# Seven quarter-block products for the second FFN product of the last five chunks, and token tiles that wait in DRAM

## The chip, the cores and the metric

One core of a Trainium2 chip runs the whole program in one launch. The metric is device time in microseconds (us), the median of the runs; lower is better. TensorE (PE) multiplies matrices into PSUM, VectorE (DVE) and ScalarE (ACT) read PSUM and SBUF, GpSimd (POOL) works on SBUF, and SyncE's queue (SP) issues all the DMAs of this kernel.

## What is computed

Attention with 32 pooled memories per head, then a Fourier mix over tokens and channels, then a normalised feed-forward network (FFN) with a residual:

```
a = softmax(phi over tokens);  k_m, v_m = a^T k, a^T v          # 32 memories per head
x = softmax(q k_m^T / 8) v_m                                    # (8, 576, 512)
u = x + real(fft(fft(x, tokens), channels))
un = (u - mean(u)) / sqrt(var(u) + 1e-6)
out = u + relu(un @ w_ch1) @ w_ch2                              # 512 -> 2048 -> 512
```

There are 8 batches of 576 tokens, so 4608 tokens, or 36 tiles of 128.

## The kernel before

**Two streams.** The FFN works on chunks of CH = 2 tiles (256 tokens): 18 chunks, 0 to 17, each in NW = 8 steps j of 256 hidden units. Beside it runs a generator, `background`, that makes the mixed token tiles `u` batch by batch: pooling, scores, spectrum `at`, values `vh`, and the products `pp` and `px` (`mix_m`, `mix_x`, `add_mix`). It yields 14 times per batch, and `advance` (L1134) runs it one part further per step of the FFN, as long as the ring of NU = 8 tiles (`uring`) has room; a tile is freed when its chunk is done.

**Numbers in halves.** From chunk 1 on every fp32 factor is split into an fp16 value and an fp16 rest, and a product is three matmuls: value by value, value by rest, rest by value.

**One step of the FFN.** `ffn1` (L846) makes 256 hidden units for 256 tokens: 24 matmuls of 128x256 into `ph` (they appear at L288, the line of the recording helper), then ACT writes relu as fp16 into `hring` (L864) and DVE the rest (L865). `ffn2` (L870, matmul at L874) multiplies them with `w2s`: 12 matmuls of 128x512 into two PSUM tiles `po`, one per token tile, each over all 512 output columns. ffn1 runs NHS = 7 steps ahead of ffn2. After step 7 `finish` (L882) adds `po` to `u` on DVE (L886) and sends the tile out (L887); `norm_chunk` (L792) normalises chunk c+2: ACT (L781, L782, L807), POOL (L787, and L808 for the fp16 rest `ud`), DVE (L783 to L788), and a DMA transpose into `unring`.

**Order.** A scheduler of the build sets the order of the instructions on each engine from the order of the program and its own estimate; on the chip each engine takes its queue strictly in that order and waits on semaphores. What two engines do at a time is not fixed otherwise.

```
for n in range(NW, n_steps):
    c, j = divmod(n, NW)
    ffn2(c, j, hs[c], po)
    run_ffn1(n + NHS)
    if j < NW - 1:
        advance(CH * c, steps=1)
    else:
        finish(c, po)
        if c + 2 < n_chunks:
            advance(CH * (c + 1), CH * (c + 3))
            unTs[c + 2] = norm_chunk(c + 2)
```

The functions that the diff touches, with the line numbers of the profile:

Of the kernel before, what the change touches and what calls it, by code (L numbers as in the profile page):

```python
# [10 lines left out]
F32 = mybir.dt.float32  # L11
F16 = mybir.dt.float16
# [3 lines left out]
AF = mybir.ActivationFunctionType  # L16
ALU = mybir.AluOpType
# [114 lines left out]
def kernel(  # L134
# [11 lines left out]

    const = ctx.enter_context(tc.tile_pool(name="const", bufs=1))
    psg = ctx.enter_context(tc.tile_pool(name="psg", bufs=4, space=PSUM))
    ps1 = ctx.enter_context(tc.tile_pool(name="ps1", bufs=2, space=PSUM))
    ps2 = ctx.enter_context(tc.tile_pool(name="ps2", bufs=2, space=PSUM))  # L150

# [91 lines left out]
    kept = []  # L243
# [582 lines left out]
    def h_slot(c, j):  # L826
        return hring[:, (4 + c * NW + j) % NW]
# [18 lines left out]
    def ffn1(c, unT, j, hs):  # L846

        ph = ps1.tile([P, UB, CH, P], F32, tag="h", name=f"ph_{c}_{j}")
        mm = groups()
        for f in range(UB):  # L850
            i = 0
            for k in range(NK):
                for lw, lu in ((0, 0), (0, 1), (1, 0)):
                    mm(
                        ph[:, f],
                        lhsT=w1t[:, j, lw, k, f * P : (f + 1) * P],
                        rhs=unT[:, lu, :, k],
                        start=(i == 0),
                        stop=(i == 3 * NK - 1),
                    )  # L860
                    i += 1
        h = h_slot(c, j)
        phv = ph.rearrange("p f t c -> p (f t) c")
        nc.scalar.activation(h[:, 0], phv, AF.Relu)  # L864
        nc.vector.scalar_tensor_tensor(  # L865
            out=h[:, 1], in0=phv, scalar=0.0, in1=h[:, 0], op0=ALU.max, op1=ALU.subtract
        )
        hs.append(h)

    def ffn2(c, j, hs, po):  # L870
        for f in range(UB):
            for t in range(CH):
                for i, (lh, lw) in enumerate(((0, 0), (0, 1), (1, 0))):
                    nc.tensor.matmul(  # L874
                        po[t],
                        lhsT=hs[j][:, lh, f * 2 + t],
                        rhs=w2s[:, j * UB + f, lw, :],
                        start=(j == 0 and f == 0 and i == 0),
                        stop=(j == NW - 1 and f == UB - 1 and i == 2),
                    )  # L880

    def finish(c, po):  # L882
        for t in range(CH):
            idx = CH * c + t
# [116 lines left out]
    n_chunks = n_tiles // CH  # L1001

    allocs = []

    def background():

        nt = 0
        u2, half_made = None, None
        for b in range(B):
            n = f"{b}"  # L1010
            ivs = tiny("ivs", NG)
            mem, ahl = {}, {}
            if b != 1:
                pooling_weights(b)
            yield (nt if half_made is None else half_made), 0
            if b == 0:

                for g in range(NG + 1):
                    if g < NG:
                        km = memory_f32(b, g, first[g], vmf, [0])  # L1020
                        mem[g] = first[g][:, KV:], None, km, 1.0 / 8.0
                    if g > 0:
                        ahl[g - 1] = pair_scores(b, g - 1, *mem.pop(g - 1), aeo)
                for g in range(NG):
# [17 lines left out]
            vbd = vbdt.rearrange("p (l g) f -> p l g f", l=2)  # L1042
            for g in sorted(ahl):
                pair_transpose(b, g, ahl.pop(g), attnT)
            full = slice(0, P)
            for t in (0, 1, 2) if b % 2 == 0 else (2, 0, 1):
                yield (nt if half_made is None else half_made), 2 if t < 2 else 1 - b % 2
                if t == 2:
                    if b % 2 == 0:
                        u2 = uring[:, len(allocs) % NU]  # L1050
                        us[nt] = u2
                        allocs.append(nt)
                        half_made = nt
                        nt += 1
                    rows = slice(64 * (b % 2), 64 * (b % 2) + 64)
                    tm = mix_m(b, "t2", slice(256, 320), rows, at, vh, isg, isq)
                    px = mix_x(b, "t2", 4 * P + 64, 64, rows, attnT, vbd)
                    add_mix(u2, rows, px, igx, tm, 0)
                    half_made = nt - 1 if b % 2 == 0 else None
                    continue  # L1060
                tm = mix_m(b, f"t{t}", slice(t * P, (t + 1) * P), full, at, vh, isg, isg)
                for sign in range(2):
                    c0 = (2 * t + sign) * P
                    px = mix_x(b, f"t{t}{sign}", c0, P, full, attnT, vbd)
                    u = uring[:, len(allocs) % NU]
                    allocs.append(nt)
                    add_mix(u, full, px, igx, tm, sign)
                    us[nt] = u
# [113 lines left out]
    unTs[2] = norm_chunk(2)  # L1182
    for n in range(NW, n_steps):
        c, j = divmod(n, NW)
        if j == 0:
            po = [ps2.tile([P, 512], F32, tag="o", name=f"po_{c}_{t}") for t in range(CH)]
        ffn2(c, j, hs[c], po)
        run_ffn1(n + NHS)
        if j < NW - 1:
            advance(CH * c, steps=1)  # L1190
        else:
            finish(c, po)
            if c + 2 < n_chunks:
# [66 lines left out]
```

## Time and profile before

| what | us |
|---|---|
| median of 3 runs (lowest to highest) | 943.62 (942.4 to 962.26) |
| the profiled execution's own time | 943.25 |
| its span, from the first to the last instruction | 941.4 |
| PE busy in the span | 931.6 |

A duration in the rows is that of one instruction on its engine, waiting on another engine's use of a shared resource included. Matmuls are pipelined: the duration of one is longer than the distance to the next, so rates are read from runs of many. "Idle before" is the time in which the engine stood still ahead of a group, with what ended it. POOL spans are rough.

### The profile page before, as it was taken

Reading aid. Unit: us, or ns where it says so; the run is one execution under the profiler, and the core shown is the slowest. Engines: PE = TensorE matmul, PEld = TensorE weight load, DVE = VectorE, ACT = ScalarE, POOL = GpSimd, SP = SyncE. Lnnn points to the kernel's source line nnn. Section 1 sums busy time; section 2 is a strip of 40 time slices with the busy share of each in tenths; the row PEclk is TensorE's granted clock in tenths of the full one; section 3 lists DMA queues with packets and bytes.
Section 4 is the critical chain, followed back from the end, with each engine's and each line's share of the span. In section 5 each row is a group of like instructions: output and inputs, shape, how many; then the busy total and the mean of one; then the engine's idle time right before and its main releaser. Section 6 shows DMA issues by size and latency. Waiting matters only on the chain.

```text
span 941.4 us, 18994 instructions
## 1 busy us (share of the span) xinstructions
PE 931.6 (99%) x7820; PEld 666.2 (71%) x7820; DVE 548.0 (58%) x1271; ACT 459.6 (49%) x920; POOL 217.5 (23%) x255
## 2 busy tenths in 40 slices
PE   9999899999999999999999999999999999999998
PEld 8977577676777777676767767777776767666664
DVE  5989957576656666667514766667656675221111
ACT  5668858655465536554514554656446444311110
POOL 1313424142212314223100331323122231200000
PEclk9999899999999999999999999999999999999999
DMA  9957521642235412553104531373124211110000
GB/s 328 383 217 245 184 85 24 124 123 68 53 75 123 105 42 46 141 111 93 24 23 86 115 103 42 59 162 98 26 68 85 72 25 47 23 46 23 1 24 22
DMA packets 115959, 88.09 MB, mean 94 GB/s; under 512 B 100384, under 2 KB 100384, under 8 KB 113824
## 3 DMA queue, kind: packets, MB, share of 16 engines
q1 hardware_dynamic: 115872, 86.87, 34.7%
q8 instruction: 61, 1.00, 0.4%
q14 instruction: 26, 0.21, 0.1%
HBM read 58.15 MB, written 9.44 MB: 72 GB/s over the span
## 4 chain that ended last, share of the span: by engine, by line
PE 88%; DVE 3%; ACT 1%; issue 1%; POOL 0%; DVEq 0%; ACTq 0%
PE ph L288 38%; PE po L874 37%; PE pm L288 2%; PE pp_t L288 2%; PE px_t L288 2%; PE psc L288 1%; PE po L838 1%; PE pa L684 1%; DVE w2s L930 1%; PE ph L821 1%; PE pv L657 1%; PE pp_t L727 1%; PE pf L362 1%; DVE w1t L930 0%; ACT elt L941 0%
## 5 line engine op out<-in xcount | busy, mean ns | idle before, releaser
L288 PE MATMUL ph<-unring,w1t 128*128 128x256 f16 x3264 | 388.9, 273 | 0.0
L874 PE MATMUL po<-w2s,hring 128*128 128x512 f16 x1632 | 378.8, 379 | 0.0
L288 PEld LDWEIGHTS <-w1t 128*128 128x128 f16 x3264 | 315.0, 98 | 64.4 <-issue 3.3
L874 PEld LDWEIGHTS <-hring 128*128 128x128 f16 x1632 | 156.8, 98 | 158.0 <-issue 0.4
L865 DVE SCALAR_TENSOR_TENSOR hring<-ph,hring 128x512 f16<-128x512 f32 x136 | 93.1, 685 | 155.4 <-ACT hring L864 154.8
L864 ACT ACTIVATE hring<-ph 128x512 f16<-128x512 f32 x136 | 80.3, 591 | 161.3 <-PE ph L288 160.9
L592 POOL TENSOR_TENSOR aring<-aring,scratch 128x384 f32<-128x384 f32 x28 | 23.3, 833 | 212.2 <-DVE scratch L590 208.6
L787 POOL TENSOR_TENSOR scratch<-scratch,small 128x1 f32<-128x1 f32 x36 | 21.7, 608 | 168.2 <-DVE scratch L786 135.1
L288 PEld LDWEIGHTS <-stg 128*128 128x128 f16 x1152 | 44.8, 98 | 8.4
L586 ACT ACTIVATE aring<-aring,scratch 128x384 f32<-128x384 f32 x24 | 14.7, 612 | 71.0 <-DVE aring L585 71.0
L808 POOL TENSOR_TENSOR ud<-un,ud 128x1024 f16<-128x1024 f32 x17 | 36.2, 2129 | 29.6 <-ACT ud L807 27.7
L509 POOL TENSOR_TENSOR stg<-rawt,stg 128x640 f16<-128x640 f32 x12 | 17.7, 1475 | 90.2 <-ACT rawt L508 90.2
L838 PE MATMUL po<-w2s,hring 128*128 128x512 f32 x64 | 32.8, 637 | 4.3 <-ACT hring L824 4.2
L611 ACT CAST aeo<-eo 128x384 f16<-128x384 f32 x30 | 15.3, 511 | 41.4 <-DVE eo L608 41.4
L886 DVE SCALAR_TENSOR_TENSOR uring<-po,small,uring 128x512 f32<-128x512 f32 x34 | 24.0, 742 | 17.6 <-PE po L874 17.6
L576 DVE TENSOR_REDUCE scratch<-psc 128x12 f32<-128x384 f32 x32 | 17.6, 549 | 28.5 <-PE pm L288 16.1
L763 DVE SCALAR_TENSOR_TENSOR uring<-px_t,scratch,share 128x256 f32<-128x256 f32 (+1 forms) x80 | 33.9, 475 | 0.2 <-PE px_t L288 0.2
L602 POOL TENSOR_TENSOR aring<-aring 128x128 f32<-128x128 f32 x56 | 32.8, 605 | 2.1
L604 DVE TENSOR_TENSOR eo<-aring 128x128 f32<-128x128 f32 x29 | 29.5, 1018 | 5.9 <-POOL aring L602 5.9
L288 PE MATMUL pm<-et,stg 128*128 128x64 f16 (+1 forms) x740 | 32.0, 195 | 0.0
L821 PE MATMUL ph<-unring,w1t 128*128 128x256 f32 x128 | 32.0, 395 | 0.0
L749 DVE SCALAR_TENSOR_TENSOR share<-pp_t,scratch,small 128x257 f32<-128x257 f32 (+1 forms) x48 | 21.0, 480 | 18.1 <-ACT small L746 18.0
(263 smaller groups left out, 1212.3 us busy)
## 6 DMA issues: line engine op xcount, KB each, us to landing
out<-uring SPq DMA_DIRECT2D x36, 256.0 KB, 2.1
rawt<-in_raw SPq DMA_DIRECT2D x13, 640.0 KB, 4.9
stg<-in_raw SPq DMA_DIRECT2D x13, 640.0 KB, 4.8
stg<-in_w SPq DMA_DIRECT2D x7, 1024.0 KB, 6.0
rawt<-in_raw SPq DMA_DIRECT2D x15, 384.0 KB, 3.3
stg<-in_raw SPq DMA_DIRECT2D x15, 384.0 KB, 3.1
phs<-in_raw SPq DMA_DIRECT2D x28, 160.0 KB, 3.8
w2s<-in_w SPq DMA_DIRECT2D x4, 1024.0 KB, 10.8
```

Source lines behind the costliest of these rows:

```text
L288: m = nc.tensor.matmul(out, lhsT=lhsT, rhs=rhs, start=start, stop=stop)
L592: eng.tensor_tensor(out=a, in0=a, in1=sm.unsqueeze(2).to_broadcast([P, 12, M]), op=ALU.mult)
L602: eng.tensor_tensor(out=a2[:, i : i + 4], in0=a[:, 0:4], in1=a[:, 4:8], op=op)
L604: nc.vector.tensor_tensor(out=eo[:, 1:3, 0], in0=ap[:, 1:3, 0], in1=ap[:, 1:3, 1], op=ALU.add)
L763: nc.vector.scalar_tensor_tensor(out=u[rows, hs], in0=px[rows, hs], scalar=igx[rows], in1=tm[rows, w * NJ + half : w * NJ + half + 256], o ...
L808: marks[f"ul{c}"] = nc.gpsimd.tensor_tensor(out=ud[:, 1], in0=un, in1=ud[:, 0], op=ALU.subtract)
L821: nc.tensor.matmul(ph, lhsT=w[:, k, f * P : (f + 1) * P], rhs=unTs[0][:, k], start=(k == 0), stop=(k == NK - 1))
L838: nc.tensor.matmul(po[t], lhsT=h[:, f, t], rhs=w[:, f], start=(j == 0 and f == 0), stop=(j == NW - 1 and f == UB - 1),)
L864: nc.scalar.activation(h[:, 0], phv, AF.Relu)
L865: nc.vector.scalar_tensor_tensor(out=h[:, 1], in0=phv, scalar=0.0, in1=h[:, 0], op0=ALU.max, op1=ALU.subtract)
L874: nc.tensor.matmul(po[t], lhsT=hs[j][:, lh, f * 2 + t], rhs=w2s[:, j * UB + f, lw, :], start=(j == 0 and f == 0 and i == 0), stop=(j == NW ...
L886: nc.vector.scalar_tensor_tensor(out=u, in0=po[t], scalar=cout if c else 0.5, in1=u, op0=ALU.mult, op1=ALU.add)
```

## The change

Three things are done together.

1. **Seven products.** For chunks 13 to 17 (from C0 on) the second product is written with 2 x 2 blocks: the two token tiles by the two 128-unit halves of a step, against the two halves by two blocks of 256 output columns. Instead of eight block products there are seven, of sums and differences of blocks (the scheme of Strassen in Winograd's form). A step then has 21 matmuls of 128x256 (L960) in place of 12 of 128x512. The factors have to be made: four sums of blocks of `w2s` for each j, once (`prepare_sums` on POOL, L910 to L915; `split_sums`, a copy on ACT, L920, and a subtraction on DVE, L921), and four sums of blocks of relu(ph) for each step (`ffn1_sums`: relu on ACT, L927, four 128x128 operations on DVE, L929, a 128x896 copy on ACT, L930, and a 128x896 subtraction on DVE, L931). `finish_sums` puts the seven products together (L977, L979, L983 to L987). In chunk 17 the products p2, p4 and p3 of steps 4 to 7 come last.
2. **Tiles in DRAM.** Mixed tiles from number 10 on are written to one of two slots of `uring`, sent to `kept_u` in DRAM (`keep`, L1129), and fetched for their chunk (`fetch`, L1135), so that the ring no longer stops the mixing. `due` gives it one part per step, eight per chunk instead of seven, and it must be through at the end of chunk 11.
3. **Places.** The operands of 1 lie in buffers of the mixing: the fp16 weight sums `t_slots` in `stg` and `rawt`, the sums of activations `s_slots` in `phs`, `et`, `aeo`, `attnT` and `hring`, two fp32 buffers `sums` in `aring` and `vh`, and two fp32 buffers `t_sums` for the weight sums in `at` and `uring[:, 2:4]`. ffn1 runs NS - 1 = 6 steps ahead from chunk 13 on.

```
+    t_sums = [flat(at, "a c").bitcast(F32)[:, : 2 * DM].rearrange("p (f c) -> p f c", f=UB), uring[:, 2:4]]
...
+        if c >= C0:
+            hs.append(ffn1_sums(c, j, ph))
+            return
...
+    def prepare_sums(j):
+        w, t, N = w2s[:, j * UB : (j + 1) * UB], t_sums[j % 2], DM // 2
+        nc.gpsimd.tensor_tensor(out=t, in0=w[:, :, 0], in1=w[:, :, 1], op=ALU.add)
+        b11, b12, b21, b22 = (t[:, f, n * N : (n + 1) * N] for f in range(2) for n in range(2))
+        nc.gpsimd.tensor_tensor(out=b11, in0=b12, in1=b11, op=ALU.subtract)
+        nc.gpsimd.tensor_tensor(out=b12, in0=b22, in1=b12, op=ALU.subtract)
+        nc.gpsimd.tensor_tensor(out=b22, in0=b22, in1=b11, op=ALU.subtract)
+        nc.gpsimd.tensor_tensor(out=b21, in0=b21, in1=b22, op=ALU.subtract)
+    def split_sums(j):
...
+        nc.scalar.copy(out=hi, in_=tf)
+        nc.vector.tensor_tensor(out=lo, in0=tf, in1=hi, op=ALU.subtract)
+    def ffn1_sums(c, j, ph):
+        m = (c - C0) * NW + j
+        a, h = sums[m % 2], s_slots[m % NS]
+        nc.scalar.activation(a[:, 0:4], ph.rearrange("p f t c -> p (f t) c"), AF.Relu)
+        for o, x, y, op in ((6, 1, 0, ALU.subtract), (4, 0, 2, ALU.add), (5, 2, 6, ALU.subtract), (7, 3, 5, ALU.subtract)):
+            nc.vector.tensor_tensor(out=a[:, o], in0=a[:, x], in1=a[:, y], op=op)
+        nc.scalar.copy(out=h[:, 0], in_=a[:, 1:8])
+        nc.vector.tensor_tensor(out=h[:, 1], in0=a[:, 1:8], in1=h[:, 0], op=ALU.subtract)
...
+        factors = {
+            "p1": (0, plain(0, 0)),
+            "p6": (4, summed(3)),
...
+        for n in names:
+            a, b = factors[n]
+            for i, (la, lb) in enumerate(((0, 0), (0, 1), (1, 0))):
+                    m = nc.tensor.matmul(po[n], lhsT=h[:, la, a], rhs=b[lb],
...
+    def keep(nt, u, rows):
+        if nt >= KEPT:
+            nc.sync.dma_start(out=kept_u[nt, rows], in_=u[rows])
...
+            ffn2_sums(j, hs[c][j], po, FIRST if late else FIRST + SECOND)
...
+        if 0 < n - (C0 - 1) * NW <= NW:
+            split_sums(n - (C0 - 1) * NW - 1)
+        if c == C0 - 1:
+            prepare_sums(j)
+        run_ffn1(n + (NHS if n + NHS <= C0 * NW else NS - 1))
+        if made < n_tiles:
+            due += PACE
```

On POOL the last rows of the mixing, of which the kernel before has these ahead of its last tiles' normalisation (aring and aeo hold the scores, L787 and L808 belong to the normalisation):

```order
L592 TENSOR_TENSOR aring<-aring,scratch 128x384
L602 TENSOR_TENSOR aring<-aring 128x128 x2
L600 TENSOR_TENSOR ahring<-aring,ahring 128x5x64
L612 TENSOR_TENSOR aeo<-eo,aeo 128x8x32
L787 TENSOR_TENSOR scratch<-scratch,small 128x1
L808 TENSOR_TENSOR ud<-un,ud 128x1024
```

are followed in the changed kernel by the weight sums of j = 0 alone (in `at`) and then of two j at a time (in `uring` and `at`):

```order
L634 TENSOR_TENSOR aeo<-eo,aeo 128x8x32
L910 TENSOR_TENSOR at<-w2s 128x1024
L912 TENSOR_TENSOR at<-at 128x256
L913 TENSOR_TENSOR at<-at 128x256
L914 TENSOR_TENSOR at<-at 128x256
L915 TENSOR_TENSOR at<-at 128x256
L910 TENSOR_TENSOR uring<-w2s 128x1024
L912 TENSOR_TENSOR uring<-uring 128x256
L910 TENSOR_TENSOR at<-w2s 128x1024
L913 TENSOR_TENSOR uring<-uring 128x256
```

So 40 new POOL instructions stand in one row at the seam of chunks 12 and 13, and the normalisation of chunk 14 (two L809, one L830) stands among them.

On DVE the end of a chunk late in the kernel before reads as follows: one row per step for the rest of the activations (L865) and two rows that finish the chunk (L886).

```order
L865 SCALAR_TENSOR_TENSOR hring<-ph_3_9654,hring 128x512
L865 SCALAR_TENSOR_TENSOR hring<-ph_4_9693,hring 128x512
L886 SCALAR_TENSOR_TENSOR uring<-po_0_9369,small,uring 128x512
L886 SCALAR_TENSOR_TENSOR uring<-po_1_9370,small,uring 128x512
L865 SCALAR_TENSOR_TENSOR hring<-ph_5_9732,hring 128x512
```

At the seam of chunks 12 and 13 the changed kernel has these (et, aeo and attnT hold the activations of chunk 13, steps 1 to 3; stg takes the weight sums of j = 0 to 2; po_0 and po_1 are those of chunk 12):

```order
L929 TENSOR_TENSOR vh<-vh 128x128 x4
L931 TENSOR_TENSOR et<-vh,et 128x896
L921 TENSOR_TENSOR stg<-at,stg 128x1024
L929 TENSOR_TENSOR aring<-aring 128x128 x4
L931 TENSOR_TENSOR aeo<-aring,aeo 128x896
L929 TENSOR_TENSOR vh<-vh 128x128 x4
L998 SCALAR_TENSOR_TENSOR uring<-po_0_8825,small,uring 128x512
L921 TENSOR_TENSOR stg<-uring,stg 128x1024
L998 SCALAR_TENSOR_TENSOR uring<-po_1_8826,small,uring 128x512
L931 TENSOR_TENSOR attnT<-vh,attnT 128x896
L921 TENSOR_TENSOR stg<-at,stg 128x1024
```

One DVE row per step has become five, and at this seam six; the finish of chunk 12 (L998) and the weight rests (L921) share the queue with them.

## Rows read from the trace of the kernel before

**Rows 1.** The page: the span, and each engine's busy time, its share of the span and its instructions.

```profile
span 941.4 us, 18994 instructions
PE 931.6 (99%) x7820; PEld 666.2 (71%) x7820; DVE 548.0 (58%) x1271; ACT 459.6 (49%) x920; POOL 217.5 (23%) x255
```

**Rows 2.** Busy time of each engine in stretches of the span: the stretch, its length, then busy us (and instructions) of PE, PE's weight loads, DVE, ACT and POOL, then PE's granted clock, the DMA share and GB/s.

```profile
250.00:340.00 90.00, 90.00 (x826) 63.60 (x824) 56.56 (x133) 48.73 (x99) 25.83 (x29) 1.00 0.39 88
680.00:770.00 90.00, 90.00 (x823) 63.32 (x821) 55.94 (x132) 46.43 (x95) 23.35 (x25) 1.00 0.28 64
815.00:920.00 105.00, 105.00 (x730) 71.27 (x729) 18.75 (x27) 12.54 (x21) 0.00 (x0) 1.00 0.07 21
```

**Rows 3.** The chain of work that ended last, in order of time (start, us, what), at the end of the mixing, in a late chunk, and at the end of the span.

```profile
796.11 0.89 PE px_t L288 x16
797.00 6.69 PE po L874 x31
803.69 5.24 PE ph L288 x48
...
838.68 2.59 PE po L874 x12
841.27 2.62 PE ph L288 x24
...
922.04 14.91 PE po L874 x69
936.95 0.03 issue
936.97 0.75 DVE uring L886
```

**Rows 4.** Groups of instructions on PE: line, engine, operation, out<-in, shapes, count, then busy us and mean ns of one, then idle time before them.

```profile
L288 PE MATMUL ph<-unring,w1t 128*128 128x256 f16 x3264 | 388.9, 273 | 0.0
L874 PE MATMUL po<-w2s,hring 128*128 128x512 f16 x1632 | 378.8, 379 | 0.0
L288 PEld LDWEIGHTS <-w1t 128*128 128x128 f16 x3264 | 315.0, 98 | 64.4 <-issue 3.3
```

**Rows 5.** Instructions by line on POOL, ACT and DVE: count, then the shortest, middle and longest duration in ns, first and last start, and shapes.

```profile
L602 POOL TENSOR_TENSOR aring<-aring x56: 449/457/1053, 86.8 to 773.5; 128x128 f32<-128x128 f32 x56
L592 POOL TENSOR_TENSOR aring<-aring,scratch x28: 831/832/835, 85.9 to 772.2; 128x384 f32<-128x384 f32 x28
L808 POOL TENSOR_TENSOR ud<-un,ud x17: 2123/2130/2140, 72.7 to 810.7; 128x1024 f16<-128x1024 f32 x17
L787 POOL TENSOR_TENSOR scratch<-scratch,small x36: 549/551/1068, 50.5 to 808.0; 128x1 f32<-128x1 f32 x36
L807 ACT CAST ud<-un x17: 1028/1045/1055, 71.6 to 809.5; 128x1024 f16<-128x1024 f32 x17
L604 DVE TENSOR_TENSOR eo<-aring x29: 273/866/1473, 26.3 to 774.0; 128x128 f32<-128x128 f32 x29
L562 DVE SCALAR_TENSOR_TENSOR stg<-rawt,scratch,stg x12: 1005/1018/1470, 173.1 to 741.8; 128x768 f16<-128x768 f32 x12
L993 DVE SCALAR_TENSOR_TENSOR w2s<-w2s,small x5: 1273/1276/1817, 141.1 to 169.8; 128x1024 f16<-128x1024 f32 x5
L865 DVE SCALAR_TENSOR_TENSOR hring<-ph,hring x136: 626/690/693, 133.5 to 922.7; 128x512 f16<-128x512 f32 x136
L763 DVE SCALAR_TENSOR_TENSOR uring<-px_t,scratch,share x80: 441/474/501, 47.2 to 798.7; 128x256 f32<-128x256 f32 x64, 64x256 f32<-64x256 f32 x16
```

**Rows 6.** DVE and POOL in order of time around 190 us: start, us, engine, line, operation, out<-in, shapes, count, and in brackets the idle time before it.

```profile
188.47 0.83 POOL L592 TENSOR_TENSOR aring<-aring,scratch 128x384 f32<-128x384 f32 x1 [13.12 <-DVE scratch L590]
188.84 1.27 DVE L562 SCALAR_TENSOR_TENSOR stg<-stg,scratch 128x768 f16<-128x768 f32 x1 [0.52 <-ACT stg L561]
189.38 1.46 POOL L602 TENSOR_TENSOR aring<-aring 128x128 f32<-128x128 f32 x2
...
190.80 1.39 POOL L509 TENSOR_TENSOR stg<-stg 128x640 f16<-128x640 f32 x1
190.87 1.47 DVE L604 TENSOR_TENSOR eo<-aring 128x128 f32<-128x128 f32 x1 [0.36 <-POOL aring L602]
```

**Rows 7.** PE around the one long wait of the span: in order of time, and then its busy time and granted clock (the third number) in stretches.

```profile
109.83 3.78 PE L838 MATMUL po<-w2s,hring 128*128 128x512 f32 x4 [3.69 <-ACT hring L824]
...
110.00:113.00 3.00, 3.00 (x4) 0.50 0.00 0
113.00:116.00 3.00, 3.00 (x8) 0.51 0.28 55
116.00:119.00 3.00, 3.00 (x19) 1.00 0.40 117
```

**Rows 8.** DMA issues: out<-in, queue, kind, count, KB each, median us from issue to landing.

```profile
out<-uring SPq DMA_DIRECT2D x36, 256.0 KB, 2.1
```

More of the change, by code (lines that the diff above doesn't have):

```diff
@@ L51 @@
 NW = NF // UB
+C0 = 13
+NS = 7
+PACE = 1.0
+KEPT = 10
 UW = UB * DM
@@ L58 @@
 W2_STAGE = ["b10", "b14", "s2", "b10", "b14", "x", "s2", "s1"]
+FIRST, SECOND = ["p1", "p6", "p7", "p5"], ["p2", "p4", "p3"]
 HEADS = [0, 1, 2, 3, 7, 6, 5, 4]
@@ L148 @@
     psg = ctx.enter_context(tc.tile_pool(name="psg", bufs=4, space=PSUM))
+    kept_u = ctx.enter_context(tc.tile_pool(name="kept", bufs=1, space=bass.MemoryType.DRAM)).tile(
+        [B * S // P, P, DM], F32, name="kept_u"
+    )
     ps1 = ctx.enter_context(tc.tile_pool(name="ps1", bufs=2, space=PSUM))
@@ L219, with flat @@
     share = const.tile([P, 2 * NJ], F32, name="share")
+    def flat(t, names):
+        return t.rearrange(f"p {names} -> p ({names})")
+    t_slots = [stg[:, i, k * 2048 : (k + 1) * 2048] for i in (0, 2) for k in range(2)]
+    t_slots += [rawt.bitcast(F16)[:, k * 2048 : (k + 1) * 2048] for k in range(2)]
+    t_slots += [stg[:, 1, k * 2048 : (k + 1) * 2048] for k in range(2)]
+    t_slots = [t.rearrange("p (l b c) -> p l b c", l=2, b=4) for t in t_slots]
+    s_slots = [flat(phs, "t g c").bitcast(F16), flat(et, "g l t c"), flat(aeo, "l t e h c"), flat(attnT, "g t c")]
+    s_slots += [flat(hring[:, i : i + 2], "a l f c") for i in (4, 6, 0)]
+    s_slots = [t[:, : 14 * P].rearrange("p (l b c) -> p l b c", l=2, b=7) for t in s_slots]
+    sums = [flat(aring, "a t m")[:, : 8 * P], flat(vh, "l k c").bitcast(F32)]
+    sums = [t.rearrange("p (b c) -> p b c", b=8) for t in sums]
+    t_sums = [flat(at, "a c").bitcast(F32)[:, : 2 * DM].rearrange("p (f c) -> p f c", f=UB), uring[:, 2:4]]
     rings, taken = {}, [0]
@@ new lines, in split_sums @@
+    def split_sums(j):
+        hi, lo = (t_slots[j][:, l].rearrange("p b c -> p (b c)") for l in range(2))
+        tf = t_sums[j % 2].rearrange("p f c -> p (f c)")
+        nc.scalar.copy(out=hi, in_=tf)
[8 more added lines that the diff above has]
+        nc.vector.tensor_tensor(out=h[:, 1], in0=a[:, 1:8], in1=h[:, 0], op=ALU.subtract)
+        return h
@@ new lines, in sums_banks, with ffn2_sums, plain, summed @@
+    def sums_banks(c):
+        banks = [ps2.tile([P, 512], F32, tag="o", name=f"po_{c}_{i}") for i in range(2)]
+        banks += [psg.tile([P, 512], F32, tag="g", name=f"po_{c}_{2 + i}") for i in range(2)]
+        names = ("p1", "p2"), ("p6", "p7"), ("p5", "p3"), ("p4",)
+        return {n: banks[i][:, k * 256 : (k + 1) * 256] for i, p in enumerate(names) for k, n in enumerate(p)}
+    def ffn2_sums(j, h, po, names):
+        def plain(f, n):
+            return [w2s[:, j * UB + f, l, n * 256 : (n + 1) * 256] for l in range(2)]
+        def summed(b):
+            return [t_slots[j][:, l, b] for l in range(2)]
+        factors = {
+            "p1": (0, plain(0, 0)),
+            "p6": (4, summed(3)),
+            "p7": (5, summed(1)),
+            "p5": (3, summed(0)),
+            "p2": (2, plain(1, 0)),
+            "p4": (1, summed(2)),
+            "p3": (6, plain(1, 1)),
+        }
+        for n in names:
+            a, b = factors[n]
+            for i, (la, lb) in enumerate(((0, 0), (0, 1), (1, 0))):
+                with tc.issue_after(marks["ps"].ins) if i == 0 and "ps" in marks else nullcontext():
+                    m = nc.tensor.matmul(
+                        po[n],
+                        lhsT=h[:, la, a],
+                        rhs=b[lb],
+                        start=(j == 0 and i == 0 and n in ("p1", "p6", "p5", "p4")),
+                        stop=(j == NW - 1 and i == 2),
+                        skip_group_check=True,
+                    )
+            marks["ps"] = m
@@ new lines, in finish_sums, with add @@
+    def finish_sums(c, po):
+        u2, u1 = us.pop(CH * c), us.pop(CH * c + 1)
+        lo, hi = slice(0, 256), slice(256, 512)
+        c1, x1 = share[:, 0:256], share[:, 256:512]
+        x2, x3 = (elt.rearrange("p l c -> p (l c)").bitcast(F32)[:, i * 256 : (i + 1) * 256] for i in range(2))
+        def add(o, p, x):
+            nc.vector.scalar_tensor_tensor(out=o, in0=po[p], scalar=cout, in1=x, op0=ALU.mult, op1=ALU.add)
+        nc.scalar.activation(c1, po["p1"], AF.Copy, scale=cout)
+        add(x1, "p6", c1)
+        add(x2, "p7", x1)
+        add(x3, "p5", x1)
+        nc.gpsimd.tensor_tensor(out=u1[:, lo], in0=u1[:, lo], in1=c1, op=ALU.add)
+        nc.vector.tensor_tensor(out=u2[:, hi], in0=u2[:, hi], in1=x2, op=ALU.add)
+        add(u2[:, hi], "p5", u2[:, hi])
+        nc.vector.tensor_tensor(out=u1[:, hi], in0=u1[:, hi], in1=x3, op=ALU.add)
+        nc.vector.tensor_tensor(out=u2[:, lo], in0=u2[:, lo], in1=x2, op=ALU.add)
+        add(u1[:, lo], "p2", u1[:, lo])
+        add(u2[:, lo], "p4", u2[:, lo])
+        nc.sync.dma_start(out=out[CH * c], in_=u2)
+        add(u1[:, hi], "p3", u1[:, hi])
+        nc.sync.dma_start(out=out[CH * c + 1], in_=u1)
@@ L1003, with place, fetch @@
     allocs = []
+    places = [0]
+    def place(nt):
+        if nt >= KEPT:
+            places[0] += 1
+            return uring[:, 2 + places[0] % 2]
+        us[nt] = uring[:, len(allocs) % NU]
+        allocs.append(nt)
+        return us[nt]
+    def keep(nt, u, rows):
+        if nt >= KEPT:
+            nc.sync.dma_start(out=kept_u[nt, rows], in_=u[rows])
+    def fetch(c):
+        for idx in range(CH * c, CH * c + CH):
+            if idx >= KEPT and idx not in us:
+                us[idx] = uring[:, (4, 5, 6, 7, 0, 1)[(idx - KEPT) % 6]]
+                nc.sync.dma_start(out=us[idx], in_=kept_u[idx])
     def background():
@@ L1049, in background @@
                     if b % 2 == 0:
-                        u2 = uring[:, len(allocs) % NU]
-                        us[nt] = u2
-                        allocs.append(nt)
+                        u2 = place(nt)
                         half_made = nt
                         nt += 1
+                    elif nt - 1 >= KEPT:
+                        u2 = place(nt - 1)
                     rows = slice(64 * (b % 2), 64 * (b % 2) + 64)
@@ L1058, in background @@
                     add_mix(u2, rows, px, igx, tm, 0)
+                    keep(nt - 1, u2, rows)
                     half_made = nt - 1 if b % 2 == 0 else None
@@ L1064, in background @@
                     px = mix_x(b, f"t{t}{sign}", c0, P, full, attnT, vbd)
-                    u = uring[:, len(allocs) % NU]
-                    allocs.append(nt)
+                    u = place(nt)
                     add_mix(u, full, px, igx, tm, sign)
-                    us[nt] = u
+                    keep(nt, u, full)
                     nt += 1
@@ L1182 @@
     unTs[2] = norm_chunk(2)
+    due = 0.0
     for n in range(NW, n_steps):
@@ L1185 @@
         if j == 0:
-            po = [ps2.tile([P, 512], F32, tag="o", name=f"po_{c}_{t}") for t in range(CH)]
-        ffn2(c, j, hs[c], po)
-        run_ffn1(n + NHS)
-        if j < NW - 1:
-            advance(CH * c, steps=1)
+            po = sums_banks(c) if c >= C0 else [
+                ps2.tile([P, 512], F32, tag="o", name=f"po_{c}_{t}") for t in range(CH)
+            ]
+        if c >= C0:
+            late = c == n_chunks - 1 and j >= NW // 2
+            ffn2_sums(j, hs[c][j], po, FIRST if late else FIRST + SECOND)
+            if late and j == NW - 1:
+                for p in SECOND:
+                    for i in range(NW // 2, NW):
+                        ffn2_sums(i, hs[c][i], po, [p])
+        else:
+            ffn2(c, j, hs[c], po)
+        if 0 < n - (C0 - 1) * NW <= NW:
[5 more added lines that the diff above has]
+            due += PACE
+        if j < NW - 1:
+            if int(due):
+                advance(CH * c, steps=int(due))
+            due -= int(due)
+            if j > 2 and c + 2 < n_chunks and made >= CH * (c + 3):
+                fetch(c + 2)
         else:
-            finish(c, po)
+            (finish_sums if c >= C0 else finish)(c, po)
             if c + 2 < n_chunks:
-                advance(CH * (c + 1), CH * (c + 3))
+                advance(CH * (c + 1), n_tiles if c == C0 - 2 else CH * (c + 3))
+                fetch(c + 2)
                 unTs[c + 2] = norm_chunk(c + 2)
```

## The prediction

> **What bounds the kernel now.** The order of reading was: the page's list of engines, the stretches, the chain, the groups on PE, the lines with their shortest and longest durations, and last single pieces of the timeline. The list of engines says PE: 931.6 of 941.4 us busy, the next engine, DVE, 58% [rows 1]. A share can hide waits, so the stretches come next: in the middle of the span and late in it PE is busy for the whole of each stretch at granted clock 1.00, its faster level of 2.4 GHz, while DVE has 63% in the middle and 18% after the mixing [rows 2]. The chain agrees: at the end of the mixing, in a late chunk and up to the last instruction it consists of PE alone [rows 3]. So time is saved only by fewer or shorter matmuls, and any wait that the change gives PE is paid in full.
>
> Rates come from the same chain: 48 ph matmuls (128x256) in 5.24 us are 109 ns each, 24 in 2.62; 12 po matmuls (128x512) take 2.59, 216 ns each [rows 3]. The groups show 273 and 379 ns for one, which is a duration and not the distance to the next, and weight loads of 98 ns [rows 4]; at 109 ns from one matmul to the next, each with its own load, the load is hidden behind the matmul ahead of it.
>
> **Seven products.** In five chunks of eight steps, 12 matmuls of 2.59 us become 21 of 128x256, 21 x 2.62/24 = 2.29 us. That is 40 x 0.2975 = **-11.9 us**, if operands are in time. The bounds are narrow: each new matmul has the shape, type and number of weight loads of a ph matmul.
>
> The Trainium skill ("TensorE: Matmul & The Clock Gate", section "The mechanism") says that a weight load overlaps matmuls in flight only when the row groups differ. Full 128-row matmuls don't differ in them, so 98 + 109 = 207 ns each would make a step 4.35 us. The row of 48 in 5.24 us speaks against that.
>
> **Weight sums at the seam of chunks 12 and 13.** Here are 40 new POOL instructions, eight units of one 128x1024 and four 128x256. The row for 1024 is 2.13 us (L808); for 256 I take 0.64, between 0.45 at 128 columns (L602) and 0.83 at 384 (L592) [rows 5]. A unit is 2.13 + 4 x 0.64 = 4.69, eight are 37.5. Chunk 14's normalisation stands among them on POOL, 2 x 0.55 (L787) + 2.13 = 3.23: 40.7 us. Then the last unit is split: ACT 1.04 (as L807), DVE 1.28 (as L993) [rows 5]; 43.1 us after the last mixed tile has freed `at`.
>
> PE meanwhile has, by the new order, 16 px (0.89), 7 ph (0.76), three more po steps (7.77), three ph steps (7.86), p1 (0.33) and 11 ph (1.20) to the first use of a weight sum: 18.8 us. Seven steps of 2.29 + 2.62 = 4.91 later it needs the last: 53.2 us. With nothing in the way, the sums are 10 us early.
>
> Something is in the way. The same DVE subtraction of two SBUF tiles (L604) takes 0.27 us at best and 1.47 at worst [rows 5]. In the piece of timeline it starts at 190.87 beside a POOL instruction that ends at 190.80 + 1.39 = 192.19, and ends at 190.87 + 1.47 = 192.34 [rows 6]: it waited that instruction out. POOL's L602 likewise stretches from 0.45 to 1.05, while L865, one of whose inputs lies in PSUM, stays at 626 to 693 beside everything [rows 5]. So two-input SBUF operations of DVE and POOL's take turns here.
>
> The Trainium skill says the same against this change ("SBUF — State Buffer", "Who interferes with whom"): a DVE instruction with two SBUF inputs and a GpSimd instruction that reads SBUF exclude each other for the whole of an instruction. By this rule nothing of the new DVE work (L929, L931, L921) runs beside the weight sums, where L865 did.
>
> POOL then also pays DVE's turns. A 128x896 subtraction lies between L562 (1.01 at 768) and L993 (1.27 at 1024) [rows 5], 1.14; less the 0.14 or so of a turn that lies beside the other engine, 1.0. Nine of them fall among the 40 instructions, and seven weight rests of 1.15: 9 + 8.1 = 17.1. The four short DVE operations fit where POOL restarts anyway; I add nothing for them. POOL ends at 40.7 + 17.1 = 57.8, the split at 60.1: 6.9 late. There are two `t_sums`, so unit j+2 also waits until DVE has split unit j. In four units I count that turnaround: 1.04 + 1.28 less the 0.64 which the other unit still has to do, 1.7 each, 6.7 in all. Last unit at 66.8, **+13.6 us** of waiting on PE. Bounds: 0 (the 10 us suffice) and about 30 (second rival).
>
> **Clock.** In the only long wait of before, 3.69 us, the granted clock is 0.50 (1.2 GHz) for the next 6 us and then 1.00 again [rows 7]; such a wait costs another 6/2 = 3.0. Units 5 and 6 stand behind the normalisation and its 3.23 us, so one wait of this length is likely: **+3.0** (bounds 0 and 6, for two).
>
> **Denser mixing.** Eight parts per chunk for seven, in the six batches 2 to 7. If all of DVE's work scaled, its 63% became 72%; ACT 54% to 62%, POOL 29% to 33% [rows 2]. Their average leaves PE covered, and the cost can only come from single turns: at most one of 1.47 - 0.27 = 1.2 in each batch, 7 us; at least 0. I take **+1.0**, near the lower end, since the row of the stretch shows no PE wait at all today.
>
> **Costed at nothing.** The trip through DRAM: 256 KB take 2.1 us to land [rows 8], the queue has two more transfers per late tile, and a tile is fetched about one chunk (39 us) before use; if that cover went, 2.1 + 2.1 per chunk. SP issues nothing that waits behind a fetch except output stores. The end of a chunk with seven products: p1 of the next waits for the reads of the banks, four of 128x256 at 0.47 (L763) [rows 5] = 1.9 us, behind 29 ph matmuls, 3.2 us; uncovered it would be 1.9 in each of four chunks. ffn1 six steps ahead instead of seven: 6 x 4.9 us is far more than relu, four 0.27, a copy of 1.0 and a rest of 1.14. POOL is nearly empty there, so no turns.
>
> **Tail.** After the last matmul one 128x256 operation (0.47) stands instead of a 128x512 one of 0.75 [rows 3, 5]: **-0.3**. Below nothing elsewhere: the ring no longer holds the mixing back, but PE never waited for it.
>
> **Sum.** On the profiled execution's own 943.25 (span 941.4 and 1.85 around it): 943.25 - 11.9 + 13.6 + 3.0 + 1.0 - 0.3 = 948.65. The median of the runs is 0.37 above that execution, so **949.0**. With 8 to 20 us of lateness, the likeliest case's own range is 943 to 956.
>
> **Rivals.**
> 1. *The sums are in time.* For it: 10 us of slack before turns, and the turns are inferred from short operations. Against it: turns plus ring take 24 us. Without waits and clock loss 943.25 - 11.9 + 1.0 - 0.3 + 0.37 = 932.4, range 930 to 938.
> 2. *Slower: DVE falls behind too.* Six two-input operations per step stand on DVE at the seam. If each waits out one POOL instruction (4.69/5 = 0.94 on average), a step takes 6 x 0.94 + 4 x 0.27 + 1.14 + 1.28 - 6 x 0.14 = 8.3 us against PE's 4.91; then activations are late as well as weights, 3.39 x 8 = 27.1 us. With the clock's 3.0: 943.25 - 11.9 + 27.1 + 3.0 + 1.0 - 0.3 + 0.37 = 962.5, range 957 to 975. It is slower than before by over 2% from 30 us of waits and clock on. Against it: most L604 do not show the longest value; the middle one is 866.
> 3. *Denser mixing makes PE wait, and the sums are in time.* Two turns of 1.47 in each of six batches, 17.6: 943.25 - 11.9 + 17.6 - 0.3 + 0.37 = 949.0. Against it: the averages above.
> 4. *The products don't get cheaper.* Loads not hidden: 40 x (4.35 - 2.59) = +70, some 1014. Only the page named under the seven products speaks for it.
>
> **How the numbers follow.** Forecast 0.56, rivals 0.25, 0.12, 0.06 and 0.01. Two per cent, about what a measurement of this kernel can tell from no change, is 18.9 us: 924.7 and 962.5. Faster needs the first rival and some 8 us more than it promises: 0.02. Slower has over half of the second rival, the fourth and the forecast's upper tail: 0.10. The rest, 0.88, is within. The range leaves out a little of the first rival below 931 and most of the second above 961: 931 to 961.
>
> **What would show it.** In the profile after: 21 po matmuls per step at 2.29 us in chunks 14 to 17, with PE at 1.00 and without waits (else rival 4); PE waits for the weight sums (ACT L920 or DVE L921) in chunks 12 to 13, 8 to 20 us in all, with a clock below 1.00 behind the longest; POOL L910 to L915 above 2.13 and 0.64, DVE L929 above 0.27 while these run, and not later. No PE wait at the seam means that rival 1 holds and my turns were wrong; waits for L927 to L931 there mean rival 2; waits before 700 us for the mixing mean rival 3. A time below 931, or PE waits at the chunk ends 14 to 17, would be outside all cases.

## The result

The changed kernel takes 956.64 us (median of 4 runs, 953.55 to 958.36) against 943.14 before: a ratio of 1.0146, 95% interval [1.0133, 1.0159]. Some executions of a kernel take about 2% longer than its others, at a lower granted clock where that was recorded (0.98); one of before is among them, without it the median before is 942.67, and the medians of the experiments below leave them out. The time lies in the range and the change is within 2%, but it is slower by 14.0 us (13.5 by the medians of all runs) where 5.4 were forecast. The profiled execution took 958.36, 15.1 more than that of before.

The page after has PE's share down, though PE has less work than before (answers to [rows 1]):

```profile
span 956.6 us, 20189 instructions
PE 928.6 (97%) x8180; PEld 704.3 (74%) x8180; DVE 650.7 (68%) x1479; ACT 501.2 (52%) x973; POOL 268.1 (28%) x300
```

The stretches show where PE stands still: after [rows 2] the columns are length, then busy us (and instructions) of PE, PE's loads, DVE, ACT and POOL, PE's granted clock, DMA share, GB/s.

```profile
250.00:340.00 90.00, 89.18 (x829) 63.24 (x828) 58.77 (x137) 49.22 (x104) 27.09 (x30) 1.00 0.44 109
650.00:700.00 50.00, 47.94 (x437) 33.32 (x435) 30.30 (x75) 28.87 (x59) 14.06 (x17) 0.97 0.38 87
760.00:780.00 20.00, 17.74 (x147) 14.91 (x146) 17.92 (x23) 7.97 (x13) 16.33 (x15) 0.91 0.11 20
780.00:800.00 20.00, 12.93 (x90) 9.95 (x88) 16.72 (x21) 8.57 (x11) 12.42 (x12) 0.74 0.04 7
815.00:920.00 105.00, 105.00 (x964) 94.10 (x963) 57.34 (x142) 40.30 (x62) 8.27 (x8) 1.00 0.10 27
```

Late chunks are clean, the seam (760 to 800) is not, and there are losses before it. PE's list of waits names them (engine, line, waited for; us in all, times, longest us):

```profile
PE po L960 <- ACT rawt L920: 5.9, 1, 5.9
PE po L860 <- ACT hring L846: 4.2, 2, 3.7
PE pm L310 <- DVE stg L535: 3.6, 2, 1.8
PE po L960 <- DVE stg L921: 2.3, 1, 2.3
PE po L960 <- DVE uring L998: 1.9, 1, 1.9
...
PE po L960 <- DVE rawt L921: 1.2, 1, 1.2
PE pm L310 <- ACT stg L528: 0.8, 2, 0.6
PE pm L310 <- DMA et<-elt: 0.8, 1, 0.8
```

L860 is the start's wait, which is in before too [rows 7]; the other rows shown are new. Four rows (L960) belong to the seam, and three (pm) to the mixing long ahead of it.

The sum can be checked from the starts of the matmuls in both traces: the distance to the next start, less the distance that this kind of matmul has when undisturbed, is what waits and a slow clock cost.

| part | forecast | measured |
|---|---|---|
| seven products (steady chunks 39.3 for 41.7 us) | -11.9 | -12.0 |
| seam: waits and slow clock, 738 to 802 us (17.1 less 1.2 before) | +16.6 | +16.0 |
| mixing: 150 to 738 us (15.3 less 6.3 before) | +1.0 | +9.0 |
| before 150 us | 0 | +0.9 |
| after 802 us | 0 | +0.2 |
| end: from the last matmul's start to the end of the span (5.44 for 4.24) | -0.3 | +1.2 |
| sum | +5.4 | +15.3 (profiled runs: 15.1) |

So the mixing's term is wrong by 8 us, and that of the end by 1.5.

**The products.** The chain in a late chunk, against [rows 3]:

```profile
829.26 2.62 PE ph L310 x24
831.88 2.29 PE po L960 x21
834.17 2.62 PE ph L310 x24
```

21 matmuls take the 2.29 us that were worked out for them, where 12 took 2.59.

**The seam.** In order of time, DVE and POOL while a weight sum is made (start, us, engine, line, shapes, count, idle before):

```profile
758.70 3.89 DVE L929 TENSOR_TENSOR aring<-aring 128x128 f32<-128x128 f32 x4
758.86 2.12 POOL L910 TENSOR_TENSOR at<-w2s 128x1024 f32<-128x1024 f16 x1 [1.16 <-DVE stg L921]
760.94 0.77 POOL L913 TENSOR_TENSOR uring<-uring 128x256 f32<-128x256 f32 x1
761.67 0.77 POOL L912 TENSOR_TENSOR at<-at 128x256 f32<-128x256 f32 x1
762.41 0.77 POOL L914 TENSOR_TENSOR uring<-uring 128x256 f32<-128x256 f32 x1
```

Four short subtractions of DVE last 3.89 us, three of them ending 0.15 us after a POOL instruction ends: the turns of [rows 6]. From 743 to 788 us seven steps take between 1.01 and 5.79 us for these four; in a late chunk, without POOL's sums, they take 1.02. POOL's L910 had waited 1.16 us for DVE's L921, the ring of two `t_sums`. PE's granted clock behind the longest wait is that of [rows 7]:

```profile
788.00:794.00 6.00, 4.48 (x21) 0.50 0.00 0
794.00:800.00 6.00, 6.00 (x48) 0.83 0.00 0
```

**The mixing.** The chain that ends in the two waits of pm at 507 and 510 us begins with a store (start, us, what):

```profile
495.81 2.05 DMA out<-uring
...
497.88 2.65 DMA uring<-kept_u
...
500.56 0.73 ACT un L803 x2
...
501.31 0.82 ACT un L804 x2
...
505.03 0.55 DVE un L810
...
507.14 1.98 DVE scratch L665
...
509.26 0.74 DVE stg L535
...
510.04 0.61 PE pm L310 x15
```

The output of chunk 7 leaves, then the tiles of chunk 10 are fetched into its slots, and the normalisation of chunk 10 stands on ACT and DVE right behind that, a chunk before its place in the program: the build has pulled it up, as soon as a slot comes free. ACT there, in order of time (in brackets the idle time before, and what ended it):

```profile
500.56 0.63 ACT L803 ACTIVATE un<-uring 128x512 f32<-128x512 f32 x1 [3.02 <-DMA uring<-kept_u]
...
504.86 0.62 ACT L608 ACTIVATE aring<-aring,scratch 128x384 f32<-128x384 f32 x1 [1.28 <-DVE aring L607]
...
506.80 1.55 ACT L528 ACTIVATE stg<-stg,scratch 128x640 f16<-128x640 f32 x2
```

What pm needs (L528 on ACT, L535 on DVE) is queued behind the normalisation. Of all ACT's waits for a fetch the trace has

```profile
ACT un L803 <- DMA uring<-kept_u: 16.9, 11, 3.1
```

and before there is no fetch. Near the end of the same chain DVE's L665, with a single column, takes 2 us: it waits out POOL's L830, a part of the same normalisation. So the turns have a part here too.

```profile
506.97 2.13 POOL L830 TENSOR_TENSOR ud<-un,ud 128x1024 f16<-128x1024 f32 x1 [1.98 <-ACT ud L829]
507.05 2.06 DVE L665 TENSOR_TENSOR scratch<-scratch,small 128x1 f32<-128x1 f32 x1
```

### The profile page after: what moved, and what is told of

It is laid out like the page before. It is cut to its first block, busy times and chain, and to the rows that moved or that the text cites. A ratio compares the mean times of both kernels' runs of the same rounds, so it can differ in the third digit from the quotient of the medians.

```text
span 956.6 us, 20189 instructions
## 1 busy us (share of the span) xinstructions
PE 928.6 (97%) x8180; PEld 704.3 (74%) x8180; DVE 650.7 (68%) x1479; ACT 501.2 (52%) x973; POOL 268.1 (28%) x300
## 4 chain that ended last, share of the span: by engine, by line
PE 59%; DVE 7%; ACT 3%; DMA 2%; issue 1%; POOL 0%; SPq 0%; ACTq 0%; DVEq 0%; POOLq 0%
PE ph L310 26%; PE po L899 17%; PE po L960 8%; PE pm L310 2%; DVE aring L929 1%; PE pp_t L310 1%; PE px_t L310 1%; PE psc L310 1%; DMA out<-uring 1%; DVE vh L929 1%; PE pa L706 1%; DMA uring<-kept_u 1%; DVE stg L921 1%; DVE rawt L921 0%; PE pp_t L749 0%
## 5 line engine op out<-in xcount | busy, mean ns | idle before, releaser
L310 PE MATMUL ph<-unring,w1t 128*128 128x256 f16 x3264 | 397.0, 274 | 0.0
L899 PE MATMUL po<-w2s,hring 128*128 128x512 f16 x1152 | 268.3, 379 | 0.0
L899 PEld LDWEIGHTS <-hring 128*128 128x128 f16 x1152 | 111.2, 98 | 111.1 <-issue 0.9
L890 DVE SCALAR_TENSOR_TENSOR hring<-ph,hring 128x512 f16<-128x512 f32 x96 | 65.4, 682 | 18.0 <-ACT hring L889 16.8
L889 ACT ACTIVATE hring<-ph 128x512 f16<-128x512 f32 x96 | 56.4, 588 | 29.3 <-PE ph L310 28.9
L809 POOL TENSOR_TENSOR scratch<-scratch,small 128x1 f32<-128x1 f32 x36 | 21.8, 609 | 148.7 <-DVE scratch L808 142.6
L310 PEld LDWEIGHTS <-stg 128*128 128x128 f16 x1152 | 44.2, 98 | 11.9 <-DVE stg L535 4.0
L830 POOL TENSOR_TENSOR ud<-un,ud 128x1024 f16<-128x1024 f32 x17 | 37.2, 2187 | 32.9 <-ACT ud L829 31.1
L929 DVE TENSOR_TENSOR aring<-aring 128x128 f32<-128x128 f32 x80 | 30.4, 417 | 13.0 <-ACT aring L927 12.3
L960 PEld LDWEIGHTS <-hring 128*128 128x128 f16 x336 | 33.7, 100 | 6.1 <-issue 1.4
L929 DVE TENSOR_TENSOR vh<-vh 128x128 f32<-128x128 f32 x80 | 27.3, 380 | 15.6 <-ACT vh L927 14.6
L633 ACT CAST aeo<-eo 128x384 f16<-128x384 f32 x30 | 15.3, 510 | 42.1 <-DVE eo L630 41.9
L860 PE MATMUL po<-w2s,hring 128*128 128x512 f32 x64 | 32.8, 636 | 4.3 <-ACT hring L846 4.2
L983 POOL TENSOR_TENSOR uring<-uring,share 128x256 f32<-128x256 f32 x5 | 3.7, 730 | 112.8 <-ACT share L979 112.8
```

The costliest lines, as they stand in the source:

```text
L310: m = nc.tensor.matmul(out, lhsT=lhsT, rhs=rhs, start=start, stop=stop)
L809: nc.gpsimd.tensor_tensor(out=rs, in0=rs, in1=half, op=ALU.pow)
L830: marks[f"ul{c}"] = nc.gpsimd.tensor_tensor(out=ud[:, 1], in0=un, in1=ud[:, 0], op=ALU.subtract)
L860: nc.tensor.matmul(po[t], lhsT=h[:, f, t], rhs=w[:, f], start=(j == 0 and f == 0), stop=(j == NW - 1 and f == UB - 1),)
L890: nc.vector.scalar_tensor_tensor(out=h[:, 1], in0=phv, scalar=0.0, in1=h[:, 0], op0=ALU.max, op1=ALU.subtract)
L899: nc.tensor.matmul(po[t], lhsT=hs[j][:, lh, f * 2 + t], rhs=w2s[:, j * UB + f, lw, :], start=(j == 0 and f == 0 and i == 0), stop=(j == NW ...
```

## The experiments

All kernels compute the whole result. In those with two constants more, lines are two higher (L805 is L803 of the changed kernel). "Before", run beside them, had medians of 942.1 to 942.9 us.

**What does the mixing cost without the seam?** e1 has no seven products and no weight sums; e2 has seven parts per chunk; e3 has eight, spread evenly.

```
e1:  -C0 = 13
     +C0 = 18            (no chunk comes to it; two new constants keep
                         the weight sums and the early end of the mixing out)
e2:  as e1, -PACE = 1.0
            +PACE = 0.875
e3:  as e1, in the last step of a chunk:
            +if int(due) and made < n_tiles:
            +    advance(CH * c, steps=int(due))
            +due -= int(due)
```

> No seven products and no weight sums: all chunks as before, with the tiles in DRAM and eight parts of the mixing per chunk. In the changed kernel PE lost 8.9 us more than before ahead of the seam (of these 0 to 700 us: waits and slow clock 7.9). Theory D (eight parts per chunk are too dense on average for DVE, ACT and POOL) and theory P (two parts fall into the first step of a chunk, beside the normalisation) both expect about 952, with waits of pm for stg around 270, 507 and 667 us. Theory S (these waits belong to the seven products' program as a whole, not to the mixing) expects 943 to 945.

> As e1, with seven parts per chunk, one in each of the first seven steps, as before, but without the pause of the ring. D and P: 943 to 945, no PE wait above 0.3 us between 160 us and the end. Theory Q (the trip through DRAM itself, its transfers among those of the raw inputs and its wait for a slot) expects 948 to 952.

> As e1, eight parts per chunk, but the eighth goes into the last step of the chunk, so that no step has two. D: about 952 as e1. P: 944 to 946.

Measured: e1 950.0 (ratio 1.0080, [1.0065, 1.0095]), e2 950.67 (1.0083, [1.0066, 1.0099]), e3 951.28 (1.0094, [1.0079, 1.0109]). The loss is there without any seam, and the same at seven parts per chunk as at eight: neither density (D) nor two parts in a step (P) explains it alone, and what e1 to e3 share is the way through DRAM (Q). In e2 ACT waits for a fetch oftener and longer than in the changed kernel:

```profile
ACT un L805 <- DMA uring<-kept_u: 45.4, 18, 5.4
```

**Is it the place of the normalisation?** Its ACT instructions are put behind the relu of step 3 of the next chunk, when the fetch is done. Everything else follows e1, e2 and e3.

```
-unTs[c + 2] = norm_chunk(c + 2)
+with tc.issue_after(marks[f"r{c + 1}_3"].ins):     # relu of ffn1(c + 1, 3)
+    unTs[c + 2] = norm_chunk(c + 2)
```

> As e1 (no seven products, tiles in DRAM, eight parts per chunk), but ACT's part of the normalisation of chunk c+2 stands behind the relu of step 3 of chunk c+1, some five steps later than the build put it, long after its tiles have been fetched. Theory W (the normalisation stands at the head of ACT's and DVE's queues while its tiles are still being fetched, and what pm needs stands behind it): 943 to 945, and ACT's L805 never waits for a fetch. Theory N (unpaused mixing meets the normalisation's own work at the chunk's start, whoever waits for whom): 949 to 951.

> As e2 (no seven products, tiles in DRAM, seven parts per chunk) with the normalisation put later as in e5. In e2 each PE wait of over 0.5 us behind 500 us came 3 to 6 us after L805 had stood 3.7 to 5.1 us for a fetch. Theory W alone: 943 to 944.5. If what was left in e5 (waits of pm for et and for POOL L533) has nothing to do with eight parts per chunk, these stay: 946 to 948.

> As e3 (eight parts per chunk, the eighth in the chunk's last step, so that no step has two) with the normalisation put later. If e5's rest of 4.5 us is from two parts in one step (theory P): 943 to 945. If it is from eight parts as such (theory D): 946 to 948.

Measured: e5 947.25 (1.0046, [1.0028, 1.0064]), e9 943.67 (1.0011, [1.0001, 1.0022]), e10 947.98 (1.0060, [1.0043, 1.0077]). e5 lies between what W and N expected, so neither holds alone at eight parts. ACT's waits for a fetch are gone (0.3 us in e5, none in e9), and at seven parts per chunk PE's waits as well; e9's whole list behind 150 us is:

```profile
PE po L901 <- DVE uring L1000: 0.4, 1, 0.4
PE ph L312 <- DVE hring L892: 0.2, 1, 0.2
```

The medians side by side:

| parts per chunk | normalisation behind the fetch | later |
|---|---|---|
| 7 | 950.67 | 943.67 |
| 8 | 950.0 | 947.25 |
| 8, evenly | 951.28 | 947.98 |

At seven parts the place is worth 7.0 us and explains all but about 1 us of the trip through DRAM (W). At eight it is worth 2.75 to 3.3 and leaves 4 to 6: then eight parts cost 3.6 to 4.3 more than seven, which does not show while the fetch holds up the queues. e10 tells that two parts in one step are not the reason. In e5 PE waits elsewhere; its whole list behind 150 us is:

```profile
PE pm L312 <- DMA et<-elt: 2.8, 3, 1.5
PE pm L312 <- POOL stg L533: 1.1, 1, 1.1
```

The trace has part of the reason for `et`. Each batch has two of these transposes. In before, PE's first product with the first one starts 0.7 to 1.6 us after it has landed, with the second 4.0 to 8.3 us after. Transfers that take over 6 us from issue to landing are all the second of their batch in before (6.28 to 7.00) and in e9 (6.19 to 6.91), and PE waits for none. In e5 two of the first take that long, each issued right behind a fetch of `kept_u` and a load of raw input, and PE waits for both:

```profile
454.14 6.28 DMA et<-elt
...
651.89 7.50 DMA et<-elt
```

What makes the first ones slow with eight parts was not tested and stays open.

**Is the seam's cost lateness, and are turns its cause?** e4 makes the weight sums in the same place and uses them from chunk 14 on. e7 leaves everything as it is and gives the 40 operations to DVE.

```
e4:  -C0 = 13
     +C0 = 14             (mixing through at the end of chunk 11 and
                           weight sums in chunk 12, as in the changed kernel)
e7:  -nc.gpsimd.tensor_tensor(out=t, in0=w[:, :, 0], in1=w[:, :, 1], op=ALU.add)
     +nc.vector.tensor_tensor(out=t, in0=w[:, :, 0], in1=w[:, :, 1], op=ALU.add)
     ...                  (and the four subtractions)
```

> As the changed kernel with its weight sums and its end of the mixing in the same places (chunk 12 and chunk 11), but the seven products begin with chunk 14, a chunk of 42 us later than the weight sums. If the seam's 16 us are lateness of the weight sums alone: 943.1 - 4 x 2.4 + 8.9 + 1.5 (end) + 0.8 = 944.7, no PE wait after 750 us. Rival: the weight sums on POOL disturb DVE so much that the activations of chunk 12 and 13 come late as well: 950 to 957, PE waits for L889 to L931 there.

> As the changed kernel, with the 40 weight-sum operations on DVE in place of POOL. Theory T (DVE and POOL take turns for two-input SBUF operations, so that at the seam their times add up anyway, and DVE is the faster of the two): DVE has 1.3 + 4 x 0.41 + 1.22 + 2.2 = 6.3 us per unit, eight in 50 to 54 us, so the seam costs 2 to 7 us in place of 16: 943 to 949. Rival (no turns; the sums were late because of DVE's own queue and the ring of two): each unit burdens DVE with 2.9 us more, 956 to 966. DVE L929 at 0.27 us throughout by T.

Measured: e4 944.57 (1.0021, [1.0006, 1.0035]), where 944.7 was worked out; of the seam a wait of 1.6 us for the finish of chunk 13 is left. So the seam's cost is lateness. That it is the weight sums that are late, and not the activations, is told by PE's list of waits rather than by e4, which also takes the four short subtractions of chunk 13 from beside the weight sums: the list names L920, L921 and the finish of chunk 12 (L998), and nothing of L927 to L931. e7 takes 941.54 (0.9981, [0.9967, 0.9994]): 15.1 us gained by moving 40 operations from an engine at 28% to one at 68%. It beats its expectation; the one wait of over a microsecond at the seam is 1.6 us in the starts of the matmuls. The short subtractions in the first of the two buffers (count, shortest, middle and longest ns, first and last start, shapes), first in the changed kernel, then in e7:

```profile
L929 DVE TENSOR_TENSOR aring<-aring x80: 278/285/2221, 725.1 to 936.4; 128x128 f32<-128x128 f32 x80
```

```profile
L929 DVE TENSOR_TENSOR aring<-aring x80: 278/284/293, 725.4 to 921.3; 128x128 f32<-128x128 f32 x80
```

The longest falls from 2221 ns (a whole L910 of POOL, 2.12) to 293. DVE is full at the seam, but no longer waiting:

```profile
760.00:780.00 20.00, 20.00 (x185) 17.90 (x184) 19.56 (x43) 11.91 (x17) 14.84 (x2) 1.00 0.00 1
```

19.56 of 20 us on DVE hold 43 instructions, where 17.92 held 23 in the same stretch of the changed kernel, and PE has no gap. Without turns this would have cost time, as the rival had it. e7 changes two things at once, the turns and the speed of the sums (a 128x1024 one takes 1.22 us on DVE and 2.12 on POOL); how the 15.1 us divide between them was not separated.

**Do the parts add up to a better kernel?**

```
e6:   e4 and the later normalisation
e8:   e6, and p1, p2, p6, p7 in psg, p5, p3, p4 in ps2 (in sums_banks)
e11:  weight sums on DVE, C0 = 14, PACE = 0.9375, later normalisation for c <= 11
e12:  e7 and the later normalisation for c <= 10
```

> As e4 (seven products in four chunks, weight sums a chunk ahead) with the normalisation put later as in e5. W: 944.8 - 7.5 = 937 to 938. N: 944 to 946.

> As e6, with p1, p2, p6 and p7 in the PSUM banks that the mixing has left (four, so two sets) and p5, p3, p4 in the two of the finishing chunk. In e4 p1 of chunk 14 waited 1.6 us for the finish of chunk 13 (DVE L1000). If that wait goes and none takes its place: 1.6 below e6, 935 to 936.5; if p5 meets the same wait, as e6.

> Weight sums on DVE, seven products in chunks 14 to 17, 7.5 parts per chunk, mixing through at the end of chunk 12, normalisation later up to that of chunk 13. 942.9 - 9.6 + 1.5 (end) + 1.6 (seam, as e7) + 2 to 4 (mixing, between e9's and e5's) = 938 to 941.

> e7 (the changed kernel with the weight sums on DVE) with the normalisation put later up to that of chunk 12. 941.5 - 2.75 (as e1 to e5) = 938.8, if the seam stays as in e7; 940 to 942 if the later normalisation of chunk 12 meets the weight sums.

Measured: e6 950.09 (1.0074, [1.0058, 1.0090]) and e8 949.20 (1.0065, [1.0046, 1.0083]): e6 is outside both values expected, e8 close to e6, as its second case had it. The mixing gained, but at the start of chunk 14 there is now

```profile
PE po L962 <- DVE uring L1000: 7.6, 1, 7.6
```

where e4 had 1.6: DVE comes to the finish of chunk 13 only behind turns with POOL's weight sums, of which the last ends at 792.7 us for 782.0 in e4, and behind the normalisation put beside them. Other banks (e8) do not help, and how much each of the two holds it up was not separated. e12 is 942.73 (1.0006, [0.9996, 1.0016]), 1.2 above e7 and a little over the 940 to 942 expected if the later normalisation meets the weight sums: with the normalisation later, PE waits four times for weight sums at the seam. e11 is 939.01 (0.9962, [0.9948, 0.9976]), as expected and the fastest of all: 3.1 us below before, 17.6 below the changed kernel.

## Why the prediction went wrong

- **Seven products, -11.9: right.** 2.29 us per step; the fourth rival is out.
- **Weight sums, +13.6, and clock, +3.0: right** in mechanism: turns with POOL, shown by the rows of L929 with and without POOL's sums, and late sums, shown by PE's waits and e4. That the Trainium skill's rule ("SBUF — State Buffer", "Who interferes with whom") decides here is borne out by L929's 2221 against 293 ns. That the sum is so near (16.0 for 16.6) is partly luck. The 17.1 us are 12.4 of waits and 4.7 of slow clock, against 1.1 of waits in before: 2.3 less of the one and 1.7 more of the other than forecast. POOL's row of 40 sums lasts 63.9 us, where the forecast's terms gave 64.5, but the terms differ: 40.0 at the shortest durations (37.5 forecast), 10.3 of waits for L921 (6.7), 6.4 for the normalisation and the wait for it (3.2), and only 7.0 by which the sums are stretched (17.1). The first rival (sums in time) failed: PE waits 9.4 us for weight sums. So did the second: PE's list has no wait for activations there.
- **Denser mixing, +1.0 with 0 to 7: the step that failed, with 9.0.** It was worked out from the engines' average load and from turns alone, and the trip through DRAM stood under "costed at nothing": a tile "is fetched about one chunk (39 us) before use". It isn't. With six slots for three chunks the fetch waits until the output of the chunk three before has left, and the build puts the normalisation straight behind it, at the head of ACT's and DVE's queues. The 2.1 + 2.1 us named there for lost cover were nearly the right time for the two transfers (2.05 and 2.65 in the chain). I priced the transfer, and never asked what stands behind the instruction that waits for it. At seven parts per chunk this place costs 7.0 us. At eight, as in the changed kernel, putting it right gains 2.75 to 3.3 (measured without the seam), and 4 to 6 us stay.
- **Eight parts per chunk** cost 3.6 to 4.3 us once the normalisation is out of the way (e5 and e10 against e9), within the 0 to 7 of the forecast but not by its mechanism alone: of PE's 3.9 us of waits in e5, 2.8 are for a transfer. With the early normalisation eight parts take no longer than seven, so the two costs do not add, and the 9.0 can't be split between them. 1.7 of the 9.0 are slow clock behind one of the waits (at 670 us, below). The third rival's mechanism, a PE wait in the mixing, was real (9.0 us where it had 17.6), but I had counted it as an alternative to the forecast; both happened together.
- **Tail, -0.3: wrong, +1.2.** Not one operation follows the last matmul but five, since the seven products are put together in a chain on DVE:

```profile
951.03 0.38 PE L960 MATMUL po<-w2s,hring 128*128 128x256 f16 x2
...
951.45 0.48 DVE L977 SCALAR_TENSOR_TENSOR elt<-po,small,share 128x256 f32<-128x256 f32 x1
951.85 0.87 DVE L977 SCALAR_TENSOR_TENSOR uring<-po,small,uring 128x256 f32<-128x256 f32 x2
952.64 0.41 DVE L986 TENSOR_TENSOR uring<-uring,elt 128x256 f32<-128x256 f32 x1
...
953.09 0.48 DVE L977 SCALAR_TENSOR_TENSOR uring<-po,small,uring 128x256 f32<-128x256 f32 x1
```

## What to carry to other kernels

When a tile goes through DRAM, look where the order puts its first reader: an early place is free as long as the data are there, and turns into a wait at the head of a queue when they have to be fetched. Price a wait by what stands behind it on its engine. Two engines that take turns are one: work may be better off on the busier, if that one is faster. And mechanisms in different places of a program are no alternatives, as the seam and the mixing were not; their costs add. Two in the same place need not: take away both before you call either harmless.

## What was not expected of the hardware

Turns need not be even. In e7, with DVE issuing two-input SBUF operations back to back, one POOL instruction of the normalisation that takes 2.13 us alone [rows 5] took 19.44:

```profile
767.36 19.44 POOL L830 TENSOR_TENSOR ud<-un,ud 128x1024 f16<-128x1024 f32 x1 [3.15 <-ACT ud L829]
```

The granted clock fell behind shorter waits of PE than the 3.69 us [rows 7] that I had counted on. In the changed kernel it fell to its lower level after a wait of 1.83 us that ended at 669.40 (for DVE's L535) and after one of 2.26 that ended at 770.91 (for DVE's L921); after waits of 1.72 and 1.93, ended at 510.04 and 752.89, it stayed at 1.00.

```profile
667.00:670.00 3.00, 0.94 (x22) 0.95 0.03 6
670.00:673.00 3.00, 3.00 (x19) 0.50 1.11 194
772.20:775.40 3.20, 3.20 (x17) 0.50 0.00 0
775.60:778.00 2.40, 2.40 (x24) 1.00 0.00 0
```
